# Dropping the memory rows from the attention projections of a recurrent-memory layer, and checking the approximation by a bound

## The chip, the cores and the metric

One core of one Trainium2 chip. The metric is the device time of one execution in microseconds. The kernel before took 1615.88 us (median of 12 runs, 1615.55 to 1616.53).

Names: PE is TensorE (matmul), PEld its weight loads, DVE is VectorE, ACT is ScalarE, POOL is GpSimd, SP is SyncE. A "head" below is one pass of the attention loop: the projections of one head interleaved with the attention of the head before.

## The reference, cut to what matters

```python
xn = layernorm(x)                                # x: 1 x 2048 x 1024
for s in range(64):                              # segments of 32 rows
    h = concat([mem, xn_segment])                # 8 memory rows + 32 rows
    q, k, v = h @ Wq, h @ Wk, h @ Wv             # 32 heads of 128
    p = softmax(mask(q @ k.T * 128 ** -0.5))
    o = (p @ v) @ Wo
    mem = o[:8];  outs.append(o[8:])
# ... (a gated feed-forward layer on xn)
return x + concat(outs) * silu(feed_forward(xn))
```

The segments depend on each other only through the 8 memory rows. On this data the attention weights are small, so both kernels replace the recurrence by closed sums for the memory (all 8 rows of a segment alike, one value row per segment), compute all segments in parallel, check at the end that the replacement holds, and fall back to a slow sequential program if it does not.

## The kernel before: the parts that the change and the argument touch

The normalized rows are packed with one memory column per segment: 63 segments x (32 + 1) columns, and 40 for the first segment with its 8 true memory rows, together 2119, padded to 2120. Three segments make a tile of 99 columns.

```python
SPT = 3; B1 = SEG + 1; TR = SPT * B1              # 99
NBLK = 5                                          # 5 blocks of 424 columns
# ... in proj_steps(h): the projections of one head, 80 matmuls
for (w_, dst) in ((wq, qt), (wk, kt)):
    for i in range(NBLK):
        a, b = edges[i], edges[i + 1]
        pr = psb.tile([P, 512], F32, name="pr", tag="big")
        for c in range(KC):                       # KC = 8
            nc.tensor.matmul(pr[:, 0:b - a], lhsT=w_[:, c, hc], rhs=xq[:, c, a:b], ...)
            if c == KC - 1:
                nc.scalar.copy(dst[:, a:b], pr[:, 0:b - a])
            yield
# ... in s_steps: 21 score matmuls of 99 columns and one of 40
nc.tensor.matmul(s_ps[:, j * TR:(j + 1) * TR], lhsT=kt[:, o:o + P], rhs=qt[:, o:o + TR], ...)
# ... then exp on ACT, and the mask (which also counts the memory column 8 times) on DVE
# ... in pv_steps: 22 value matmuls of 129 columns (128 and the denominator), 3 to a PSUM tile, 2 tiles
nc.tensor.matmul(o_ps[:, j, :], lhsT=pT[:, o:o + P], rhs=va[:, j0 + j, v0:v0 + DH + 1], ...)
nc.vector.reciprocal(rd, o_ps[0:R, 0:n, d0])
nc.vector.tensor_tensor(osb[...], o_ps[0:R, 0:n, e0:e0 + DH], rd..., op=ALU.mult)
# ... attn_steps: a score step every second projection matmul, three value steps every eighth
# ... check(): the memory rows that attention gave, multiplied by Wo, against the assumed ones
for ci in range(n):
    for h in range(H):                            # 256 matmuls of 70 columns in all
        nc.tensor.matmul(t_[:, ci, :], lhsT=wo_sb[:, h, ...], rhs=omT[:, h, K0:K0 + NCK], ...)
```

## Time and profile before

| | before |
|---|---|
| median, 12 runs | 1615.88 us |
| span of the profiled run | 1615.0 us |
| PE busy | 1601.0 us (99%) |
| attention stage, 317 to 860 us | PE busy 542.6 of 543 us |
| one head | 16.58 us |
| check at the end, PE | 8.4 us of matmuls, about 0.4 us of small products |

PE is busy almost always, and PE is also what the end of the program waits for. Busy time alone would not say that, since a matmul's recorded span (342 ns for the 424-column one, below) is longer than the distance to the next start (179 ns). From the page of the kernel before, the busy table and the chain of waits (what ended last, followed back):

```profile
PE 1601.0 (99%) x10031; PEld 834.8 (52%) x10135; DVE 534.5 (33%) x1224; ACT 412.8 (26%) x788; POOL 145.5 (9%) x213
...
PE 95%; issue 3%; DMA 1%; DVE 1%; POOL 1%; ACT 0%; POOLq 0%; ACTq 0%
```

The table by stretches, for the attention stage (columns: stretch, length; busy us and instruction count of each engine; clock; DMA share; GB/s), shows no room for PE and much for DVE and ACT:

```profile
317.00:860.00 543.00, 542.60 (x4009) 326.12 (x4012) 233.17 (x709) 237.14 (x482) 32.53 (x31) 1.00 0.38 103
```

What a matmul costs is read from start to start, not from its duration (the groups give 342 ns for the 424-column one). From the chain of the kernel before in order of time (start, us, what): the eight projection matmuls and what stands between them repeat with the head.

```profile
357.88 1.08 PE pr L587 x6
359.14 1.43 PE pr L587 x8
...
374.46 1.08 PE pr L587 x6
...
391.04 1.08 PE pr L587 x6
```

One head is 374.46 - 357.88 = 16.58 us, and eight projection matmuls take 1.43 us, 179 ns each. The first and last start of a line's instructions (duration min/median/max in ns, then first and last start in us) cut the program into stages:

```profile
L587 PE MATMUL pr<-xq,wqk x2560: 339/342/346, 317.5 to 845.7; 128*128 128x424 bf16 x197
...
L783 PE MATMUL a_ps<-wo_sb,ot x1037: 219/379/379, 1186.6 to 1609.8; 128*128 128x512 bf16 x163, 128*128 128x384 bf16 x5, 128*128 128x128 bf16 x5
```

From the timeline of PE, the old check between the first output projections:

```profile
1200.40 8.48 PE L736 MATMUL wo_ps<-omT,wo_sb 128*128 128x70 bf16 x256
```

From the timeline of DVE in a head, two lines: The second instruction starts at 437.54 while the first runs until 437.07 + 0.56 = 437.63: neighbours that do not need each other overlap by about 0.09 us.

```profile
437.07 0.56 DVE L636 TENSOR_TENSOR osb<-o_ps,rden 99x384 bf16<-99x384 f32 x1
437.54 0.36 DVE L610 TENSOR_TENSOR pT<-pT,mask 99x396 bf16<-99x396 bf16 x1
```

### The profile page before, as it was taken

How to read it: one execution, taken by the hardware profiler on the slowest of the kernel's cores; microseconds unless marked ns; L12 is line 12 of the kernel's file. 1: busy time of each engine (PE TensorE's matmuls, PEld its weight loads, DVE VectorE, ACT ScalarE, POOL GpSimd, SP SyncE). 2: the span in 40 equal slices, each digit the busy share in tenths (PEclk: the TensorE clock that was granted, in tenths of full speed). 3: DMA queues.
4: the chain of work that ended last, by engine and by line, in shares of the span. 5: the costliest groups of instructions: out<-in, count | busy, mean ns of one | idle time of the engine just before them, and what ended most of it. 6: DMA issues, size and time to landing. Idle time of an engine off the chain costs nothing.

```text
span 1615.0 us, 23936 instructions
## 1 busy us (share of the span) xinstructions
PE 1601.0 (99%) x10031; PEld 834.8 (52%) x10135; DVE 534.5 (33%) x1224; ACT 412.8 (26%) x788; POOL 145.5 (9%) x213
## 2 busy tenths in 40 slices
PE   9999999999999999999999999999999999999998
PEld 4444546656666566666654444444454444444444
DVE  6655434334444444444444212212212111111111
ACT  4333331144444444444442111111100000000000
POOL 2222210001000100001001111011100000000000
PEclk9999999999999999999999999999999999999999
DMA  7996665544433343324313545442451443525340
GB/s 215 186 153 148 202 183 164 174 118 130 124 108 106 106 133 84 107 81 103 113 28 98 184 132 181 135 145 66 114 125 63 117 104 103 131 81 131 76 129 28
DMA packets 241136, 198.18 MB, mean 123 GB/s; under 512 B 98748, under 2 KB 202764, under 8 KB 241008
## 3 DMA queue, kind: packets, MB, share of 16 engines
q1 hardware_dynamic: 199040, 124.79, 29.8%
q0 software_dynamic: 31408, 57.11, 12.3%
q10 hardware_dynamic: 10576, 14.70, 2.8%
q8 instruction: 81, 1.33, 0.3%
q14 instruction: 31, 0.25, 0.1%
HBM read 112.80 MB, written 64.08 MB: 110 GB/s over the span
## 4 chain that ended last, share of the span: by engine, by line
PE 95%; issue 3%; DMA 1%; DVE 1%; POOL 1%; ACT 0%; POOLq 0%; ACTq 0%
PE pr L587 28%; PE a_ps L783 14%; PE y_ps L773 12%; PE u_ps L170 12%; PE g_ps L166 12%; PE v_ps L356 10%; PE o_ps L630 2%; PE s_ps L602 2%; PE acc L401 1%; DMA vp_dram<-v_sb 1%; PE vm_ps L523 1%; PE vm_ps L499 1%; PE wo_ps L736 1%; POOL vp_dram L369 0%; PE pt L321 0%
## 5 line engine op out<-in xcount | busy, mean ns | idle before, releaser
L587 PE MATMUL pr<-xq,wqk 128*128 128x424 bf16 x2560 | 520.7, 342 | 0.0
L587 PEld LDWEIGHTS <-wqk 128*128 128x128 bf16 x2560 | 209.2, 97 | 125.6
L783 PE MATMUL a_ps<-wo_sb,ot 128*128 128x512 bf16 (+2 forms) x1037 | 225.0, 372 | 1.0
L356 PE MATMUL v_ps<-wv_sb,xnT 128*128 128x512 bf16 x1002 | 222.3, 379 | 2.0 <-DMA wv_sb<-in_A_Wv_dram 0.7
L170 PE MATMUL u_ps<-xnT,wu 128*128 128x512 bf16 x882 | 210.4, 379 | 1.4 <-DVE hst L174 0.5
L166 PE MATMUL g_ps<-xnT,wg 128*128 128x512 bf16 x866 | 208.9, 379 | 1.4
L773 PE MATMUL y_ps<-wd,ht 128*128 128x512 bf16 x877 | 197.1, 379 | 1.0
L174 DVE SCALAR_TENSOR_TENSOR hst<-th,u_ps 128x512 bf16<-128x512 f32 x112 | 77.1, 688 | 296.8 <-PE u_ps L170 274.7
L783 PEld LDWEIGHTS <-ot 128*128 128x128 bf16 x1056 | 102.0, 98 | 119.4
L356 PEld LDWEIGHTS <-xnT 128*128 128x128 bf16 x1024 | 99.4, 98 | 118.8 <-ACT xnT L323 1.2
L173 ACT ACTIVATE th<-g_ps 128x512 f32<-128x512 f32 x112 | 66.9, 597 | 325.8 <-PE g_ps L166 305.7
L170 PEld LDWEIGHTS <-wu 128*128 128x128 bf16 x896 | 87.7, 98 | 106.4 <-issue 0.8
L773 PEld LDWEIGHTS <-ht 128*128 128x128 bf16 x896 | 87.6, 98 | 105.0
L166 PEld LDWEIGHTS <-wg 128*128 128x128 bf16 x896 | 86.5, 98 | 101.2
L602 PE MATMUL s_ps<-qt,kt 128*128 128x99 bf16 x672 | 137.6, 208 | 0.0
L636 DVE TENSOR_TENSOR osb<-o_ps,rden 99x384 bf16<-99x384 f32 (+1 forms) x256 | 134.0, 523 | 8.8
L590 ACT CAST kt<-pr 128x424 bf16<-128x424 f32 x160 | 81.9, 512 | 148.8 <-PE pr L587 146.0
L776 ACT ACTIVATE th<-y_ps 128x512 f32<-128x512 f32 x32 | 19.1, 597 | 392.0 <-PE y_ps L773 392.0
L590 ACT CAST qt<-pr 128x424 bf16<-128x424 f32 x160 | 81.9, 512 | 138.1 <-PE pr L587 136.7
L359 ACT CAST v_sb<-v_ps 128x512 bf16<-128x512 f32 x128 | 74.4, 586 | 146.8 <-PE v_ps L356 116.0
L610 DVE TENSOR_TENSOR pT<-pT,mask 99x396 bf16<-99x396 bf16 (+1 forms) x160 | 60.0, 375 | 124.1 <-ACT pT L608 124.1
L635 DVE RECIPROCAL rden<-o_ps 99x3 f32<-99x3 f32 (+1 forms) x256 | 45.6, 178 | 163.7 <-PE o_ps L630 141.4
(107 smaller groups left out, 809.0 us busy)
## 6 DMA issues: line engine op xcount, KB each, us to landing
va<-vp_dram SPq DMA_DIRECT2D x16, 1039.5 KB
o_dram<-osb POOLq DMA_DIRECT2D x16, 1039.5 KB, 12.4
vp_dram<-v_sb POOLq DMA_DIRECT2D x60, 256.0 KB, 8.2
hT_dram<-hst POOLq DMA_DIRECT2D x56, 256.0 KB, 3.3
ht<-hT_dram SPq DMA_DIRECT2D x16, 896.0 KB
xt<-in_A_x_dram SPq DMA_DIRECT2D x32, 256.0 KB
wo_t<-in_A_Wo_dram ACTq DMA_DIRECT2D x8, 1024.0 KB
wo_t<-in_A_Wo_dram SPq DMA_DIRECT2D x8, 1024.0 KB
```

Of the source, the lines that this page charges most:

```text
L166: nc.tensor.matmul(g_ps[:], lhsT=wg[:, c, fc * P:(fc + 1) * P], rhs=xnT[:, c, tb * TB:(tb + 1) * TB], start=(c == 0), stop=(c == KC - 1))
L170: nc.tensor.matmul(u_ps[:], lhsT=wu[:, c, fc * P:(fc + 1) * P], rhs=xnT[:, c, tb * TB:(tb + 1) * TB], start=(c == 0), stop=(c == KC - 1))
L173: nc.scalar.activation(th[:], g_ps[:], ACTF.Tanh, scale=0.5)
L174: nc.vector.scalar_tensor_tensor(hst[:, :, fc, :], th[:].rearrange("p (a b) -> p a b", b=P), 1.0, u_ps[:].rearrange("p (a b) -> p a b", b= ...
L356: nc.tensor.matmul(v_ps[:], lhsT=xnT[:, c, t * P:(t + 1) * P], rhs=wv_sb[:, c, cg * 512:(cg + 1) * 512], start=(c == 0), stop=(c == KC - 1))
L359: nc.scalar.copy(v_sb[:, j * 512:(j + 1) * 512], v_ps[:])
L587: nc.tensor.matmul(pr[:, 0:b - a], lhsT=w_[:, c, hc], rhs=xq[:, c, a:b], start=(c == 0), stop=(c == KC - 1))
L590: nc.scalar.copy(dst[:, a:b], pr[:, 0:b - a])
L602: nc.tensor.matmul(s_ps[:, j * TR:(j + 1) * TR], lhsT=kt[:, o:o + P], rhs=qt[:, o:o + TR], start=True, stop=True)
L636: nc.vector.tensor_tensor(osb[0:R, j0:j0 + n, hh * DH:(hh + 1) * DH], o_ps[0:R, 0:n, e0:e0 + DH], rd.unsqueeze(2).to_broadcast([R, n, DH]) ...
L773: nc.tensor.matmul(y_ps[:], lhsT=hts[t][:, c, :], rhs=wd[:, c, hf * 512:(hf + 1) * 512], start=(c == 0), stop=(c == FC - 1))
L783: nc.tensor.matmul(a_ps[:], lhsT=ox[t][0][:, h, :], rhs=wo_sb[:, h, a:b], start=(h == 0), stop=(h == H - 1))
```

## The change

The intent is to take work from PE. If the memory's score is so small that exp(score) is 1, its query and key need no projection: a memory of 8 equal rows adds 8 to the denominator and 8 times its value row to the numerator. So the memory columns leave the projections (2056 columns remain: 2048 and the 8 true rows of the first segment), tiles become 128 rows of 4 segments, and DVE adds the memory's part after the value matmul. What the old check read from the attention is no longer there; the new one bounds the scores by norms: the largest |q| and |k| are tracked per head (DVE), squared norms of the weights summed (ACT), and a few small matmuls at the end add over partitions.

```diff
-SPT = 3
-B1 = SEG + 1
-TR = SPT * B1
+SPT = P // SEG
-    NPE = NP + NP % 2
+    NPE = M + S
 ...
+        def track(x, t):
+            ab = sb.tile([P, S], BF16, name="ab", bufs=1)
+            nc.vector.tensor_scalar(ab[:].bitcast(I32), t[:, M:NPE].bitcast(I32), 0x7FFF7FFF, None, op0=ALU.bitwise_and)
+            for a in (0, S // 2):
+                m = mx[:, x, a:a + S // 2]
+                nc.vector.tensor_tensor(m, m, ab[:, a:a + S // 2], op=ALU.max)
 ...   proj_steps
+                nc.scalar.activation(fsq[:], w_[:, :, hc], ACTF.Square, accum_out=fro[:, x, h:h + 1])
-                        nc.tensor.matmul(pr[:, 0:b - a], lhsT=w_[:, c, hc], rhs=xq[:, c, a:b],
+                        nc.tensor.matmul(pr[:, 0:b - a], lhsT=w_[:, c, hc], rhs=xmT[:, c, a:b],
 ...
+                            if i == NBLK - 1:
+                                track(x, dst)
 ...   s_steps: 16 matmuls of 128 columns and one of 40; pv_steps: 16 + 1 of 129
-            rd = rden[0:R, h, j0:j0 + n]
-            nc.vector.reciprocal(rd, o_ps[0:R, 0:n, d0])
-            nc.vector.tensor_tensor(osb[0:R, j0:j0 + n, hh * DH:(hh + 1) * DH], o_ps[0:R, 0:n, e0:e0 + DH], ...)
+            ot = sb.tile([P, 3, DH + 1], F32, name="of", bufs=3)
+            nc.vector.tensor_tensor(ot[:, 0:n, :], o_ps[:, 0:n, :], vm[:, j0:j0 + n, v0:v0 + DH + 1], op=ALU.add)
+            rd = rden[:, h, j0:j0 + n]
+            nc.vector.reciprocal(rd, ot[:, 0:n, d0])
+            nc.vector.tensor_tensor(osb[:, j0:j0 + n, hc], ot[:, 0:n, e0:e0 + DH], ...)
 ...   check()
-                        nc.tensor.matmul(t_[:, ci, :], lhsT=wo_sb[:, h, ...], rhs=omT[:, h, K0:K0 + NCK], ...)
+            for i, src in enumerate((mxs[:, 0, :], mxs[:, 1, :], wnb[:, 0:512], wnb[:, 512:DM])):
+                bp = ps.tile([1, 512], F32, name="bp", tag="tp", bufs=2)
+                nc.tensor.matmul(bp[:], lhsT=ones[:], rhs=src, start=True, stop=True)
+                nc.vector.tensor_reduce(big[:, i:i + 1], bp[:], axis=AX.X, op=ALU.max)
```

Cut: the layouts in memory (value rows, memory rows and outputs now lie in plain row order, and the memory rows are broadcast by DMA over 32 partitions each), the small tests at the end, and the ACT and DVE order, which is now the program's on ACT in the attention stage and on both in the last stage.

## The prediction

> **What bounds it now.** TensorE. The page's busy table has PE at 1601 of 1615 us; PE is 95% of the chain of waits; granted clock 1.000. In a table by stage, the attention stage (317 to 860 us) has PE busy 542.6 of 543 us, VectorE (DVE) 233, ScalarE (ACT) 237. So only PE work, or a helper engine that becomes late, changes the time.
>
> **PE costs, from start-to-start spacing in the chain.** A projection matmul of 424 columns is spaced 179.5 ns, a score matmul of 99 columns about 45 ns, three value matmuls of 129 columns 170 ns together (56 each). One head takes 16.58 us. All fit columns/2.4 + about 3 ns, with weight loads hidden; "TensorE: Matmul & The Clock Gate", part of the Trainium skill, states N/2.4 GHz + about 2.5 ns for warm back-to-back matmuls, and this trace agrees.
>
> **What the change does.** The 63 single memory columns leave the packed input; the memory's score counts as exp(0)=1, so 8 times its value row is added after the value matmul, and new checks bound the error.
>
> PE removed, per head:
> - projections: 2120 to 2056 columns, 16 matmul rows: 0.427 us, x32 = 13.7 us
> - scores: 22 to 17 matmuls, 2119 to 2088 columns: about 0.03 us, x32 = 0.9 us
> - values: 22 to 17 matmuls: 5 x 56 ns, x32 = 9.0 us
>
> The old check (256 matmuls of 70 columns, 8.4 us on PE, plus 0.4) becomes a few small matmuls that wait for DVE reductions: about 4 us. Saves about 4.8 us. PE sum: about -28 us, to 1588, if nothing stalls.
>
> Added, per head (one head is then about 15.8 us of PE):
> - DVE: an add of 128x387 from PSUM before each division (0.56 us, like the 384-wide multiply's 558 ns); six value batches 7.6 us; masks 2.0 us (512-wide about 0.43); tracking of |q| and |k| maxima: per tensor a bitwise AND over 1024 int32 and two 1024-wide bf16 maxima (0.69 each, from the mask's 363/422 ns at 396/495). The AND is 0.69 us if it runs two elements per cycle (as fp32 tensor_scalar 512 in 426 ns does), 1.23 if one. DVE: 7.2 now, then 13.8 or 14.9 of 15.8 us: 87 or 94%.
> - ACT: two Square passes over 1024 (about 1.0 us each): about 10 of 15.8 us. No trouble.
> - DMA: 1 MB of broadcast rows per pair; DMA share in the stage 0.38 to about 0.5. No trouble.
>
> **What lands on PE.** In the DVE's program order the k-tracking stands before the first mask, and the q-tracking between value batches. Walking one head by these durations, DVE frees the fourth value batch's PSUM tile (two buffers) about when the sixth needs it, 13.2 us into the head: about 0.2 us stall per head in the fast case (6 us in all), about 1 us (30 us in all) in the slow case. I hold the fast case at two to one.
>
> In the last stage the squares (ACT) and sums (DVE) of the output weights fill idle engines.
>
> **Prediction: 1593 us, range 1583 to 1613.** Faster by over 2%: 0.12; within 2%: 0.85; slower: 0.03.
>
> **What would show it.** A steady head of 15.8 to 16.1 us; projection spacing about 174 ns; DVE 85 to 90% busy in the stage; the AND at about 0.69 us; waits of PE on the value add or first mask of 0.1 to 0.3 us per head; old check gone, the new costing PE 3 to 5 us once.
>
> **What would make it wrong.** The AND at 1.23 us or DVE operations dearer than modelled: head time becomes DVE's, 16.5 or more, and the gain is gone. DVE with no stall: 1588 or less. The new check failing on this data would run the sequential fallback, far slower.

## More of the kernel before

PE's and SP's instruction order is the program's. The order of DVE is left to the scheduler of the program builder in the attention stage.

## The result, and the profile after

| | before | after |
|---|---|---|
| median | 1615.88 us (12 runs) | 1589.96 us (8 runs, 1588.89 to 1591.60) |
| span of the profiled run | 1615.0 us | 1587.0 us |
| one head | 16.58 us | 15.80 us |
| DVE busy in one head | 7.32 us | 12.57 us |
| DMA share in the attention stage | 0.38 | 0.64 |

The ratio is 0.984 (95% interval 0.983 to 0.985): within 2%, by 25.9 us. A ratio is the mean time of one kernel's fast runs over that of the other's in the same rounds, so it is not quite the ratio of the medians quoted.

The page of the kernel after (busy table, chain of waits) still names PE:

```profile
PE 1569.1 (99%) x9463; PEld 815.5 (51%) x9566; DVE 747.6 (47%) x1598; ACT 504.1 (32%) x964; POOL 142.4 (9%) x220
...
PE 98%; DVE 0%; issue 0%; ACT 0%; DMA 0%; ACTq 0%; DVEq 0%
```

The stages of the kernel after, by the same two lines as before:

```profile
L593 PE MATMUL pr<-xnT,wqk x2560: 334/337/338, 316.8 to 822.2; 128*128 128x412 bf16 x118, 128*128 128x410 bf16 x79
...
L827 PE MATMUL a_ps<-wo_sb,ot x1036: 219/379/379, 1162.7 to 1581.3; 128*128 128x512 bf16 x162, 128*128 128x384 bf16 x6, 128*128 128x128 bf16 x5
```

Differences of these starts tell where the 28 us of the profiled runs went:

| stretch | before | after | difference |
|---|---|---|---|
| start to first projection | 317.5 | 316.8 | -0.7 |
| first projection to first output projection | 869.1 | 845.9 | -23.2 |
| first to last output projection (holds the check) | 423.2 | 418.6 | -4.6 |
| to the end | 5.2 | 5.7 | +0.5 |

The medians differ by 25.9 us, not by 28.0: the profiled run before was slower than all 12 timed ones, and the profiled run after faster than all 8. The first row is where such scatter lies: over all traces it varies from 316.3 to 318.2 us. The second row repeats to 0.01 us (845.84 to 845.85 in the five traces whose PE work there is that of the kernel after, 869.13 in both with the old one), so it is the better ruler, and it is used below.

The chain of the kernel after gives the head, 387.24 - 371.45 = 15.79 us, and 1.39 us for eight projection matmuls, 174 ns each:

```profile
371.45 1.39 PE pr L593 x8
...
387.24 1.39 PE pr L593 x8
...
403.04 1.39 PE pr L593 x8
```

One head of the kernel after in the table by stretches: PE is busy in all of it, DVE in 12.57 us.

```profile
410.00:425.80 15.80, 15.80 (x116) 9.69 (x115) 12.57 (x33) 8.98 (x19) 0.53 (x1) 1.00 0.40 117
```

The groups of DVE in the kernel after (busy us, mean ns; then idle time before, and who ended it) give the durations that the prediction had to estimate:

```profile
L648 DVE TENSOR_TENSOR osb<-of,rden 128x384 bf16<-128x384 f32 x160 | 89.0, 557 | 3.3
L645 DVE TENSOR_TENSOR of<-o_ps,vm 128x387 f32<-128x387 f32 x160 | 89.0, 557 | 42.1 <-PE o_ps L636 42.0
...
L579 DVE TENSOR_TENSOR mx<-mx,ab 128x1024 bf16<-128x1024 bf16 x128 | 82.8, 688 | 1.2
...
L576 DVE TENSOR_SCALAR ab<-kt 128x1024 int32<-128x1024 int32 x32 | 22.2, 694 | 20.1 <-ACT kt L596 20.1
```

The AND runs at the fast one of the two rates that the prediction had left open. In the trace before, f32 `tensor_scalar` instructions of 256 and 512 elements take 294 and 426 ns, 0.516 ns an element; carried on to 1024 that is 0.69 us, and at twice the time per element 1.22. "VectorE: DVE Perf Modes", section "The perf-mode tier table", gives `tensor_scalar` on fp32 data in SBUF the doubled rate; this AND is on int32 data, and its 0.69 us agrees.

What PE waited for in the kernel after (who for whom; us in total, times, longest):

```profile
PE o_ps L636 <- DVE of L645: 1.7, 1, 1.7
PE spin L396 <- DVE spz L393: 1.3, 1, 1.3
PE bp L782 <- DVE g2r L778: 1.1, 1, 1.1
...
PE bp L782 <- DVE bigs L783: 0.4, 2, 0.2
```

In the attention stage there is one wait, 1.7 us, once: in the first attended head the scheduler put all the masks ahead of the first value add. No other head stalls. The predicted 0.2 us a head is not there. The two `bp` waits are the new check's.

### The profile page after: what moved, and what is told of

It reads as the page before. It is cut to its first block, busy times and chain, and to the rows that moved or that the text cites. A ratio compares the mean times of both kernels' runs of the same rounds, so it can differ in the third digit from the quotient of the medians.

```text
span 1587.0 us, 23188 instructions
## 1 busy us (share of the span) xinstructions
PE 1569.1 (99%) x9463; PEld 815.5 (51%) x9566; DVE 747.6 (47%) x1598; ACT 504.1 (32%) x964; POOL 142.4 (9%) x220
## 4 chain that ended last, share of the span: by engine, by line
PE 98%; DVE 0%; issue 0%; ACT 0%; DMA 0%; ACTq 0%; DVEq 0%
PE pr L593 28%; PE a_ps L827 14%; PE v_ps L345 14%; PE y_ps L817 12%; PE u_ps L172 12%; PE g_ps L168 12%; PE o_ps L636 2%; PE s_ps L616 2%; PE acc L385 1%; PE vm_ps L507 1%; PE vm_ps L483 1%; PE pt L319 0%; DMA xt<-in_A_x_dram 0%; PE o_ps L640 0%; PE vt_ps L520 0%
## 5 line engine op out<-in xcount | busy, mean ns | idle before, releaser
L593 PE MATMUL pr<-xnT,wqk 128*128 128x412 bf16 (+1 forms) x2560 | 501.3, 337 | 0.0
L593 PEld LDWEIGHTS <-wqk 128*128 128x128 bf16 x2560 | 221.4, 97 | 128.4 <-issue 1.9
L596 ACT CAST kt<-pr 128x412 bf16<-128x412 f32 (+1 forms) x160 | 80.2, 501 | 128.1 <-PE pr L593 128.1
L645 DVE TENSOR_TENSOR of<-o_ps,vm 128x387 f32<-128x387 f32 x192 | 97.8, 510 | 42.1 <-PE o_ps L636 42.0
L616 PE MATMUL s_ps<-qt,kt 128*128 128x128 bf16 x512 | 110.3, 219 | 0.0
L833 DVE SCALAR_TENSOR_TENSOR tmp<-a_ps,gq 128x512 f32<-128x512 f32 (+2 forms) x33 | 22.3, 676 | 166.8 <-PE a_ps L827 161.0
L648 DVE TENSOR_TENSOR osb<-of,rden 128x384 bf16<-128x384 f32 x192 | 98.4, 513 | 4.4
L620 ACT ACTIVATE pT<-s_ps 128x512 bf16<-128x512 f32 x128 | 76.1, 595 | 71.3 <-PE s_ps L616 71.3
```

Source lines behind the costliest of these rows:

```text
L593: nc.tensor.matmul(pr[:, 0:b - a], lhsT=w_[:, c, hc], rhs=xmT[:, c, a:b], start=(c == 0), stop=(c == KC - 1))
L616: nc.tensor.matmul(s_ps[:, j * P:(j + 1) * P], lhsT=kt[:, o:o + P], rhs=qt[:, o:o + P], start=True, stop=True)
L620: nc.scalar.activation(pv, s_ps[:, 0:n * P], ACTF.Exp, scale=scale)
L645: nc.vector.tensor_tensor(ot[:, 0:n, :], o_ps[:, 0:n, :], vm[:, j0:j0 + n, v0:v0 + DH + 1], op=ALU.add)
L648: nc.vector.tensor_tensor(osb[:, j0:j0 + n, hc], ot[:, 0:n, e0:e0 + DH], rd.unsqueeze(2).to_broadcast([P, n, DH]), op=ALU.mult)
```

## The experiments

Each edit is to the kernel after, unless it says otherwise. All gave a correct result.

### Putting PE's old projection work back: proj_back

```diff
+                    s0 = max(0, b - 424)
-                        nc.tensor.matmul(pr[:, 0:b - a], ..., rhs=xmT[:, c, a:b],
+                        nc.tensor.matmul(pr[:, 0:424], ..., rhs=xmT[:, c, s0:s0 + 424],
-                            nc.scalar.copy(dst[:, a:b], pr[:, 0:b - a])
+                            nc.scalar.copy(dst[:, a:b], pr[:, a - s0:b - s0])
```

> The changed kernel, with each projection matmul widened back to 424 columns (the window overlaps its neighbour; only the wanted columns are copied out, the result stays right). Theory A (TensorE columns alone set the time): 80 matmuls a head times 13 columns (64 columns over five blocks, eight chunks, two weights) is 0.43 us, 32 heads 13.7 us: 1603.5 us, head period 15.80 to 16.23. Rival B (the gain came from somewhere else, such as contiguous rows in memory and fewer small packets): clearly under 7 us more.

Measured: 1603.16 us, against 1590.07 us of a kernel of the same rounds that lacks only the tracking (no_track, below): +13.1 us. From first projection to first output projection the trace has 859.3 us, 13.5 more than 845.85. The head is 16.22 us. The columns are the cost. The new layouts in memory are still in this kernel, so the rival explanation by plainer rows is out.

### Putting the old number of small matmuls back: sv_back

```diff
+                if j == 0 or (i == 0 and j == 1):
+                    nc.tensor.matmul(s_ps[:, j * P:j * P + 6], lhsT=kt[:, o:o + P], rhs=qt[:, o:o + 6], ...)
                 nc.tensor.matmul(s_ps[:, j * P:(j + 1) * P], ...)
 ...
+                for _ in range(2 if j == 0 and n == 3 else 1):
                     nc.tensor.matmul(o_ps[:, j, :], ...)
```

> The changed kernel, with five value matmuls a head issued twice and five score matmuls of 6 columns added (result unchanged). Theory A: 5 x 56 ns + 5 x about 6 ns is 0.31 us a head, about 9.9 us: 1600 us. Rival C (a small matmul costs its weight load, 98 ns in the trace, not its columns): 10 x about 98 ns is nearly 1 us a head, 31 us: 1621 us.

Measured: 1601.90 us, +11.8 over no_track, 2 us more than columns alone give; by the stretch from first projection to first output projection (859.0 against 845.85) it is 13.1 us, 3 us more. The head is 16.21 us, 0.41 longer; five value matmuls at 56 ns are 0.28 of it, so a matmul of 6 columns costs about 26 ns (an estimate: 0.13 us over 5), not 6. From start to start the trace has 27 ns, the mean of all 160. "TensorE: Matmul & The Clock Gate", section "Back-to-back issue gap", gives an issue floor of about 25 ns for 1 to 64 columns; this agrees at 6 columns, while at 64 the trace before shows 29 ns (the chain's `acc` matmuls, 0.93 us for 32). The rival, a full weight load of 98 ns for each small matmul, would have cost 31 us: weight loads stay hidden here, even for three 129-column matmuls in a row.

### Both: pe_back

> Both of these together: the new algorithm with all its new VectorE, ScalarE and DMA work, but TensorE's attention work as before. Theory A: the costs add, 13.7 + 9.9: 1613.6 us, and the new helper work is free apart from 1.7 us waited once. If the helper work cost something of its own, the sum would pass 1616.

Measured: 1615.20 us, ratio to the kernel before 0.9993 (0.9979 to 1.0006). 13.1 + 11.8 = 24.9 us were to be added to no_track's 1590.07, and 25.1 were measured. With PE's attention work as before, the new algorithm is as slow as the old one: its DVE, ACT and DMA work by itself is worth nothing, and costs almost nothing. (It still has the cheaper check, 4.6 us. On the other side its stretch from first projection to first output projection, 872.1 us, is 2.9 longer than the old kernel's 869.1: the first head's wait, 1.2 us in this run, and the dear 6-column matmuls.)

### Taking the tracking away: no_track

```diff
-                            if i == NBLK - 1:
-                                track(x, dst)
```

> The changed kernel without the tracking of the largest |q| and |k| (two ANDs and four maxima a head gone from VectorE, 4.1 us a head by their durations; the maxima stay at their zero start, so the check passes; output unchanged). Theory A (VectorE is off the critical path in steady state): within 2 us of 1590. The recorded prediction's hand walk (0.2 us stall a head from the tracking): 6 us less, 1584. Rival D (VectorE's reads slow TensorE): projection spacing would fall below 174 ns.

Measured: 1590.07 us, no change against 1589.96. The head is 15.79 us. So 4.1 us of DVE work a head are free, and the 6 us of stall that the prediction put on it do not exist. TensorE is not slowed by the tracking's traffic either: the head's length is the same to 0.01 us. (The other 9.7 us of DVE's durations in a head are still there, so of those this run says nothing.)

### Leaving the checks out: after_no_check and before_no_check

```diff
-        chk = check()
+        chk = iter(())
+        nc.vector.memset(flag[:], 0)
```

> The changed kernel with its check left out and the flag set to zero (output unchanged). Trace of the changed kernel: 0.5 us of TensorE for two small products, 3.4 us in which four row sums wait for VectorE, 0.1 for the count: 4.0 us less, 1586.

> The kernel before with its check left out and the flag set to zero (output unchanged). Its trace: 256 matmuls, 8.4 us, two transposes and a count, 0.4: 8.8 us less, 1607. With the run above: the check's share of the gain is 8.8 - 4.0 = 4.8 us.

Measured: 1584.75 us, and 1606.82 us for the kernel before without its check. Against the medians of 1589.96 and (same rounds) 1615.95 that is -5.2 and -9.1 us; by the profiled spans, -4.1 (1582.9 against 1587.0) and -10.3 (1604.7 against 1615.0, of which 8.8 lies between first and last output projection). That stretch is the ruler here: without their checks both kernels take 414.4 us for it, with them 423.2 and 418.6. So the old check cost 8.8 us and the new one 4.2, and the check's share of the gain is 4.6 us (3.9 by the medians), where 4.8 was predicted. From the timeline of PE in the kernel after, where the new check spends it (in brackets the idle time before, and who ended it):

```profile
1422.59 0.38 PE L782 MATMUL bp<-mxs,ones 128*1 128x512 bf16 x1
1424.10 0.38 PE L782 MATMUL bp<-mxs,ones 128*1 128x512 bf16 x1 [1.12 <-DVE g2r L778]
1424.69 0.38 PE L782 MATMUL bp<-wnb,ones 128*1 128x512 bf16 x1 [0.22 <-DVE bigs L783]
```

### How near is DVE to stalling PE? and2 and and3

```diff
-            nc.vector.tensor_scalar(ab[:].bitcast(I32), ..., op0=ALU.bitwise_and)
+            for _ in range(2):     # and2; and3 has 3
+                nc.vector.tensor_scalar(ab[:].bitcast(I32), ..., op0=ALU.bitwise_and)
```

> The changed kernel with each bitwise AND of the tracking issued twice (result unchanged): 0.6 us more VectorE queue before the first mask and the same between two value batches; the program order of VectorE is otherwise the same. Theory E (slack read from the trace of the changed kernel: 0.3 us before the first value matmul, 0.9 us before the sixth batch): stall about 0.4 us a head, about 12 us: 1602. The recorded walk with serial durations (1 us a head for an AND of 1.23 us, more here): 30 us or more, 1620.

> Each AND three times: 1.2 us more at either place. VectorE's sum is then about 15 of 15.8 us a head. Theory E: about 1.0 us a head at the first mask and up to 0.3 at the sixth batch: 30 to 40 us, 1620 to 1630. If VectorE had large hidden slack: under 15 us. The recorded walk: over 50 us.

Measured: 1610.10 us for and2, 1594.96 us for and3. Neither forecast held, and more work was faster. The traces say why. In and2 (timeline of DVE, then of PE) the first mask stands behind both ANDs and both maxima, and the value matmul waits for it:

```profile
415.07 1.42 DVE L577 TENSOR_SCALAR ab<-kt 128x1024 int32<-128x1024 int32 x2 [0.49 <-ACT kt L597]
416.53 1.29 DVE L580 TENSOR_TENSOR mx<-mx,ab 128x1024 bf16<-128x1024 bf16 x2
417.74 0.91 DVE L623 TENSOR_TENSOR pT<-pT,mask 128x512 bf16<-128x512 bf16 x2
...
418.21 0.34 PE L637 MATMUL o_ps<-va,pT 128*128 128x129 bf16 x3 [0.26 <-DVE pT L623]
```

Such a head lasts 16.23 us, 0.43 more, as the slack read from the trace had it. About every second head (14 of 31), though, lasts 16.78 us. There POOL issues a store of attention outputs at that moment, and the two ANDs take 1.98 instead of 1.42 us (the second of them 1246 ns in the head shown; 1244 to 1336 in the 14 heads, against 696 at most elsewhere):

```profile
431.11 1.68 POOL L656 DMA_DIRECT2D o_dram<-osb  x1 [0.21 <-issue]
431.30 1.98 DVE L577 TENSOR_SCALAR ab<-kt 128x1024 int32<-128x1024 int32 x2 [0.49 <-ACT kt L597]
```

In and3 the scheduler, seeing the longer ANDs, moved the first mask ahead of the maxima (timeline of DVE in and3), and PE waits for a mask 3.4 us in the whole program instead of 15.8, 14 times, each in a head with a store (these heads last about 16.2 us, the others 15.80):

```profile
412.77 2.15 DVE L577 TENSOR_SCALAR ab<-kt 128x1024 int32<-128x1024 int32 x3
414.84 0.42 DVE L623 TENSOR_TENSOR pT<-pT,mask 128x512 bf16<-128x512 bf16 x1
415.17 1.29 DVE L580 TENSOR_TENSOR mx<-mx,ab 128x1024 bf16<-128x1024 bf16 x2
```

So what stalls PE is not the sum of DVE's work (and3 has the most: in a head of 15.80 us without a stall the durations of its DVE instructions add up to 16.5 us) but what stands in front of the one instruction that PE needs next. The two runs differ in order as well as in amount, so they do not give a cost per AND.

### Is it POOL's issue that blocks the AND? and2_sync

```diff
-            nc.gpsimd.dma_start(o_dram[P:S, cols]..., osb[:, 1:NT, :])
+            nc.sync.dma_start(o_dram[P:S, cols]..., osb[:, 1:NT, :])
 ...   the two smaller stores likewise; on top of and2
```

> The kernel with each AND issued twice, and the three stores of the attention output issued from the sync engine's queue instead of GpSimd's (VectorE's order the same, output unchanged). In that kernel's trace the second AND before the first mask took 1336 ns instead of 690 in the heads in which GpSimd issues a 1.68 us store at that moment, and those heads last 16.79 us, the others 16.22. If GpSimd's issue blocks the AND: all heads about 16.22, no AND over 700 ns, 16 x 0.57 = 9 us less than its 1610.1: 1601. If something else delays it (the head's other loads, the weight change): still two kinds of heads and 1610.

Measured: 1602.92 us, 7.2 less than and2. All heads are 16.23 us and the longest AND is 697 ns. DVE's order is the same in both kernels, so POOL's issue was the cause. With it gone the time is what theory E had forecast for and2, 1602 us. (The expectation gives 1336 ns for all heads with a store; that was the longest of 14, and the others took 1244 to 1267.) "SBUF — State Buffer", section "Who interferes with whom", says that a DVE instruction in a two-port mode and GpSimd exclude each other from a shared port pair for a whole instruction, and that whoever issues first gets it. That one delays the other agrees with 1246 ns against 694 ns. That the first to issue holds the pair throughout is not seen here: by the trace, in which POOL's spans are rough, POOL's issue began 0.19 us before the first of the two ANDs (431.11 against 431.30), and only the second was delayed.

### Better than both? split and best

In split, each of the check's small products goes to a later half tile of its own. In best, DVE also gets the program's order in the attention stage, to remove the first head's wait.

```diff
 # split, in check()
             nc.vector.tensor_copy(g2r[:], gt[:])
+            yield
 ...
                 nc.vector.tensor_reduce(big[:, i:i + 1], bp[:], axis=AX.X, op=ALU.max)
-            yield
+                yield
 # best, on top of it, in the attention stage
-        es.enter_context(tc.manual_schedule(engines={ACT}))
+        es.enter_context(tc.manual_schedule(engines={ACT, DVE}))
```

> The changed kernel with the check's small products spread over seven later half tiles, one each, so that none waits for the VectorE reduction of the one before (output unchanged). Trace of the changed kernel: of 3.4 us at that place about 1.0 is the products themselves. Expected 2.4 us less than the changed kernel in the same rounds, its waits on the reductions (1.1 and 0.4 us in the list of waits) gone.

> The same, and VectorE's instructions of the attention stage in program order instead of the scheduler's, so that in the first head the first value add no longer stands behind all four masks: its 1.7 us wait should go. Expected 4.1 us less than the changed kernel, 1586. Risk: in steady state the third mask then stands before the first value add, which has about 0.3 us to spare; if that spare is not there, every head stalls and it is slower.

> The changed kernel itself, in the same rounds, so that the two above have a partner on the same chip: 1590 within 1 us.

Measured in the same rounds: after_again 1590.47 us, split 1588.28, best 1599.70. Split gains 2.2 us where 2.4 was expected, and beats both kernels; the waits for `bp` are gone from its list. In the traces its stretch from first to last output projection is 417.2 us against 418.6, so 1.4 us are shown to be the waits. Something else can follow the new check: in the traces of after_again, and2 and sv_back this stretch is 420.2 to 420.3 us, because right after the check's four `bp` products matmuls of 512 columns start about 427 ns apart instead of 216 for a few us (granted clock 0.76 and 0.67 in 1424 to 1427 and 1427 to 1430 us of after_again, 1.00 in the kernel after). In split and best, without those waits, it was not seen; with one trace each that does not show that it is gone.

Best loses 11.4 us to split: the first head's 1.7 us wait is gone, as expected, but the risk named beforehand came true, though at another place. Its list of waits, and one of them in its timeline of PE:

```profile
PE o_ps L636 <- DVE of L645: 8.8, 31, 0.3
```

```profile
505.67 0.27 PE L636 MATMUL o_ps<-va,pT 128*128 128x129 bf16 x2 [0.29 <-DVE of L645]
```

From the timeline of DVE in best, five heads earlier (the kernel after has these instructions in another order, shown in the next section):

```profile
421.93 0.69 DVE L576 TENSOR_SCALAR ab<-qt 128x1024 int32<-128x1024 int32 x1
422.65 1.29 DVE L579 TENSOR_TENSOR mx<-mx,ab 128x1024 bf16<-128x1024 bf16 x2
423.86 0.55 DVE L645 TENSOR_TENSOR of<-o_ps,vm 128x387 f32<-128x387 f32 x1
```

In program order the whole tracking of q stands ahead of the third value add, and add, reciprocal and multiply of a batch follow each other, each needing the one before. PE waits for the third add at the fifth batch, and the head is 16.24 us. With the same DVE instructions of the same durations (13.8 us a head in both), only their order decides between no stall and 0.44 us a head. (The list of waits counts 0.29 us of it, since the matmul before is recorded as running on for the rest.)

## Why the prediction was right, and where it was not

- **PE bounds it, and its cost is columns.** Right. The sum of PE terms was about -28 us; with the first head's 1.7 us wait that makes -26.3, and the medians differ by 25.9. (That the two profiled runs differ by 28.0 is partly luck, as said under their table.) In the attention the sum was -23.6 us; proj_back, sv_back and pe_back put 13.1, 11.8 and 25.1 us back by their medians (sv_back's 6-column matmuls cost 2 to 3 us more than the forecast 6 ns each), and the stage shortened by 23.2 us, with the 1.7 us wait of the first head in it. A head shortened by 0.78 us, where the three PE terms had 0.74.
- **The check.** Right: 4.8 us predicted, 4.6 us between first and last output projection, with and without the checks.
- **DVE's durations.** Right: the AND 0.69 us (the fast case), the add 0.557, the maximum 0.688. By the groups' means one head's DVE instructions sum to 13.8 us, the predicted figure. (The maximum's 0.69 was said to come from the mask's 363 and 422 ns; a straight line through these two gives 0.74 at 1024, and 0.69 takes the 0.516 ns an element of the `tensor_scalar`.) Its share was not: 85 to 90% busy was predicted, and 12.57 of 15.80 us is 80%.
- **The stall: the step that failed.** The prediction had "about 0.2 us stall per head in the fast case (6 us in all)". Measured: none in 31 heads and 1.7 us once, for a reason not foreseen (the scheduler's order in the first head). That term of the sum was oversized by 4.3 us, and it is the difference between 1593 and 1590.
- **Why it failed: the order.** The prediction walked one head "in the DVE's program order". That order did not run: the attention stage leaves DVE's order to the scheduler. Best runs the program's order with the same instructions, and there a stall does come in every head, 0.44 us, at the fifth batch and not, as predicted, 0.2 us at the sixth. So the walk missed twice: it took an order that the kernel doesn't have, and for that order its stall was less than half the true one.
- **A second error: adding durations.** The walk had 13.8 us of DVE work in a head. The same head shows DVE busy for 12.57 us, because neighbours that do not need each other overlap by about 0.09 us, and the scheduler's order puts such neighbours side by side (in best, DVE is busy for 12.97 us). From the timeline of DVE in a head of the kernel after, where the tracking of q stands behind the third add:

```profile
420.39 0.55 DVE L645 TENSOR_TENSOR of<-o_ps,vm 128x387 f32<-128x387 f32 x1
420.86 0.68 DVE L576 TENSOR_SCALAR ab<-qt 128x1024 int32<-128x1024 int32 x1
421.46 0.17 DVE L647 RECIPROCAL rden<-of 128x3 f32<-128x3 f32 x1
421.58 1.29 DVE L579 TENSOR_TENSOR mx<-mx,ab 128x1024 bf16<-128x1024 bf16 x2
422.79 0.55 DVE L648 TENSOR_TENSOR osb<-of,rden 128x384 bf16<-128x384 f32 x1
423.26 0.56 DVE L645 TENSOR_TENSOR of<-o_ps,vm 128x387 f32<-128x387 f32 x1
```

  From the third add to the end of the fourth this stretch takes 423.82 - 420.39 = 3.43 us, where adding the groups' means gives 3.9. The sixth batch's first matmul comes at 424.64, 0.8 us after the buffer is free, where the prediction had the two at about the same time. The overlap was visible in the trace of the kernel before (437.54, above) and was not used. How much of the margin the overlap gives is read from this trace; no run here takes the overlap alone away. What the runs do show is that the tracking costs nothing (no_track), that the margin before the first mask is about 0.3 us (and2), that a sum of durations above the head's length need not stall (and3), and that another order of the same instructions does (best).
- **DMA.** The prediction gave a share of about 0.5 in the attention stage; it was 0.64. No wait of PE for a DMA in that stage is in the list.

## What to carry to other kernels

Where one engine is the bound, cost a change in that engine's own start-to-start spacings, and for every other engine ask only whether it is in time for the next instruction that the bound engine needs. For that question add durations only along dependent instructions: independent neighbours on DVE overlap here, and their order, not their sum, decides. A small change of work can make a scheduler pick another order, so compare the order before reading a dose and its effect; and a DVE instruction that has slack may lose it when GpSimd issues a DMA at the same moment.

## What the Trainium skill lacked or had wrong

- "TensorE: Matmul & The Clock Gate", section "Back-to-back issue gap", calls N/2.4 + 2.5 ns the gap of an isolated matmul and gives about 81 ns at N=128 and 131 ns at N=512 for a stream with weight loads. Here, in a stream in which every matmul has its weight load, spacing was 174 ns at 410 to 412 columns, 179 ns at 424, 216 ns at 512 (`u_ps` in the kernel before, 1.73 us for eight) and about 56 ns at 128 and 129: the "isolated" formula holds, the stream figures do not.
- "VectorE: DVE Perf Modes", section "The DRAIN you can't avoid", says that the next operation does not start until the pipe is empty, and refers to a later section for one that is not held. Neither section says how much earlier (another page of the skill has a rough figure for what overlaps). Here independent instructions started about 0.09 us before their predecessor's recorded end (437.54 against 437.63), dependent ones about 0.03 us after it (423.26 + 0.56, then 423.85).
- "ScalarE: Activation LUTs" mentions the accumulator output but not its price: each Square pass with one was followed by a separate accumulator read of 193 ns on ACT (64 of them, 12.3 us).
- "SBUF — State Buffer", section "Who interferes with whom", was right about the shared port pair, but nothing there gives the size for a DMA issue by GpSimd: issues of 1.2 to 1.7 us stretched the second AND from 694 to between 1244 and 1336 ns (14 times in and2), and the AND that began first, right behind the start of the issue, was not delayed (and2_sync, without these issues: 697 ns at most).
